# The inverse's turn written straight into four partitions per frequency, the taps' rows in another room, and a new front order

## The chip, the cores and the metric

The kernel runs on one core of a Trainium2 chip. Its engines are TensorE (PE, with PEld its weight loads), VectorE (DVE), ScalarE (ACT), GpSimd (POOL) and SyncE (SP, which here only issues transfers); 16 DMA engines carry transfers, which are issued from the queues of SP, POOL and ACT. SBUF has 128 partitions; TensorE writes its results to PSUM. The metric is the time of one execution in microseconds. The time before is 525.67 us, the median of three runs (524.36 to 526.06).

## The reference

For x of 2048 rows and 512 columns, the result is `g * a + (1 - g) * b`, with `g = sigmoid(x . gate_w)` for each row. `b` is a dense layer pair, `gelu(x w1 + b1) w2 + b2`, 512 to 1792 and back. `a` is a state-space convolution over the 2048 rows, column by column:

```python
logdA = dt * A                                   # dt = exp(log_dt)
P = jnp.exp(logdA[:, :, None] * l[None, None, :])
K = jnp.einsum("dn,dnl,dn->dl", Cc, P, dB).real  # taps, 512 x 2048
Kf = rfft(pad(K)); Uf = rfft(pad(u)); y = irfft(Uf * Kf)[:L]
a = y + u * Dskip
```

All inputs are float32.

## The kernel before, in words

The program has two halves. The **front** computes three things side by side: the dense layers (`hidden`, then `output`, each product as three passes of a number split into a high and a low part), the 512 x 2048 taps (`taps`: `prepare`, `powers`, `magnitudes`, `rotate`, and the products of `contract` into pk), and the first stage of the transform of the input and of the taps (`first_stage`). The results of the first stages go to two arrays in DRAM, tu_d (input) and tk_d (taps): 32 blocks of 256 KB each, one for each of 32 frequencies k0. The last eighteen of the dense products of `output` (of three matmuls each) are put aside in `late`.

The order of the front's instructions on every engine is made by a planner (`Plan.run`): each task has a duration, what it reads and writes, and a due time; of the tasks that are ready on an engine the one with the earliest due time is issued. Due times come from the constants at the top of the file (T_0 and T_MLP for the dense layers, K_0 and T_KG for the taps, T_EARLY, T_LOFT and T_DEN for the loads of tu_d, and many offsets D_...), so a changed constant moves instructions on all engines.

`early` issues, at the end of the front, loads of the first tu_d blocks into rooms that the front leaves free: 8 columns of den (the room in which the taps' powers lie), 11 of attic and 8 of loft, 27 in all.

The **back** (`conv`) is written out by hand, in program order. In sixteen steps s it takes two frequencies n = 2s and 2s + 1 each: `signal` (products p2u from the tu_d rows), `taps` (products p2k from the tk_d rows, copied by ACT into k), `product` (six operations on DVE into v), `inverse` (products pa) and `turn`. `turn` copies pa to one of six tiles sa on ACT, and then has to change the layout: the last products (pb) contract over all frequencies, so that each frequency's result, [128 partitions = 2 parts c x 2 kinds x 32 q] x 512, must end up in only four partitions, with the 32 q beside each other. Before, SP writes sa to an array t_d in DRAM (t4_d in the code; 32 stores of 256 KB), and when a group of eight frequencies is there, POOL reads it back in pieces of 512 KB into 32 partitions that lie four apart: the first 8 columns q into den, the other 24 into the tile t3. The pieces of the last group are issued by ACT. The last pieces of the first two groups are held back until step 9, because their place in t3 serves for tk_d rows until then; other tk_d rows lie in a ring of eight tiles tk.

`dense` reads the dense layers' share of the output back from DRAM, 512 KB each, six times on SP in steps 7 to 12 and twice on ACT behind the last step. `rest` issues the late dense products (L1244 to L1246): three of them in step 15, the other fifteen behind the last inverse. Then come the products pb (L1304), the gate and the addition, on DVE or, for six of sixteen rows blocks, on ACT and POOL, and the stores to the output.

Of the kernel before, what the change touches and what calls it, by code (L numbers as in the profile page):

```python
# [9 lines left out]
F32 = mybir.dt.float32  # L10
# [7 lines left out]
P = 128  # L18
# [15 lines left out]
T_0 = 21.909  # L34
T_MLP = 406.545
K_0 = 31.523
T_KG = 356.763
U_0 = 28
U_GAP = 18
LAG = 12.856  # L40
TABLE = 19.14
D_KA = -33.555
D_KP = -84.187
D_S1 = 23.678
D_EV = -33.402
D_H = -65.365
D_LO = -21.589
PS = (2, 3, 1, 2)
N_ACC, N_H, N_PK, N_PU = PS
D_SP = 2.869  # L50
MEM = (6, 2, 3)
N_LD, N_HL, N_ST = MEM
D_XS = -168.313
D_G = 1.725
N_WARM = 13
T_EARLY, T_LOFT, T_DEN = 405.144, 330.334, 535.529
Y_K, Y_U = 43.23, 26.971
W_MLP = (-0.0644, -0.031, 0.0179)
W_KG = (-0.0422, -0.0319, -0.0259)
W_U = (-0.0349, -0.1398, -0.0169)  # L60
D_MAG = -0.166
D_ROT = 0.588
D_CON = 0.043
D_PHA = 0.289
D_PRE = -2.671
D_XL = 25
D_COE = -3.439
D_OUT = -2.679
N_REST = 3
D_KA0 = 0  # L70
D_DT = 19
D_PRM = -248.822
D_D0 = -601.022
D_WAVE0 = -266.408
D_COE0 = -24.094
D_SP1 = -464.705
D_G0 = 1
D_GW = 522.519
D_XS0 = 74.778
T_PRE = 0  # L80
W_CAST = (0, 0, 0, 0, 0, 0, 0, 0, 1, 1, 0, 1, 0, 0)
X_CAST = (1, 0, 1, 0)
D_X0, D_B2, D_B2C = -1509.465, -139.804, -674.499
# [30 lines left out]
def seat(n, c, kind):  # L114

    return 4 * (16 * kind + 2 * (n % 8) + c) + n // 8
# [11 lines left out]
def constants():  # L128
# [39 lines left out]
    g2 = np.zeros((32, 64, 32, 2))  # L168
    for n, k in enumerate(ko):
        er, ei = om(4 * np.outer(q - 31.5, k + 32 * k1) + (q - 31.5)[:, None])  # L170
        f2[n, 0], f2[n, 1] = er, -ei
        a = 2.0 * np.pi * (k + 32 * k1 + 0.25) / L
        g2[n, :, :, 0] = np.cos(np.outer(a, m))
        g2[n, :, :, 1] = np.sin(np.outer(a, m))
        g2[n, :, 0, 1] = 1 - 2 * (k1 % 2)
# [20 lines left out]
TURN_PE = 0.095  # L196

# [22 lines left out]
class Plan:  # L220
# [26 lines left out]
    def run(self, fixed=None):  # L247
# [13 lines left out]
        for _ in self.tasks:  # L261
# [25 lines left out]
            if t.wire:  # L287
                took, (before, behind) = t.wire
                wire = max(wire, at + before) + took
                end = wire + behind  # L290
                if p == "SP":
                    lanes.append(end)
# [13 lines left out]
def gated_mix(  # L306
# [7 lines left out]
    logdt0: bass.AP,  # L314
# [17 lines left out]
    t4_d = dr.tile([4, 2, GROUP, 2, 32, D], F32, name="t4_d")  # L332
# [11 lines left out]
    def places(attic, loft, den):  # L344

        rooms = [attic[:, k] for k in range(N_ATTIC)] + [loft[:, k * D : k * D + D] for k in range(N_LOFT)]
        return [den[:, k] for k in range(N_DEN)] + rooms + rooms[: 32 - N_US]

    def front(pool, psum, keep, attic, loft, den):
# [39 lines left out]
        pr = pool.tile([P, 6, UW], F32, name="pr")  # L389
        dtb = pool.tile([P, UW], F32, name="dtb")  # L390
# [72 lines left out]
        def early():  # L463

            us = places(attic, loft, den)
# [3 lines left out]
            for n in range(N_US):  # L469
                m = n - N_DEN  # L470
                if m < 0:
                    due, key = T_DEN + n, [("xc", n // 4)]
                elif m < N_ATTIC:
                    due, key = T_EARLY + 2.5 * m, [keys[m]]
                else:
                    due, key = T_LOFT + m, ["xt", "xv"] if m < N_ATTIC + 4 else ["tt"]
# [7 lines left out]
        def make_dt(x, k, r, ki, key, due, load, store):  # L484
# [20 lines left out]
            move(180 if n < UW else 84, load, due - 1, [], [key], hold=0.65 if n < UW else 0.4)  # L505
            vec(4 * (n + 130), before, due, [], [key])
            act(n, lambda: nc.scalar.activation(r, r, AF.Exp, scale=0.25), due, [], [key], table="exp")
            vec(6 * (n + 130), behind, due, [], [key] if store is r else [key, "dtb"])

        def first_dt():  # L510

            x, k, r, ki = (loft[:, 2048 + UW * m : 2048 + UW * m + UW] for m in range(4))
            make_dt(
                x, k, r, ki.bitcast(I32), "tt", D_D0,
                lambda: nc.sync.dma_start(x, logdt0), dtb,
            )

        def other_dts():
# [3 lines left out]
            make_dt(  # L522
                x, k, r, ki.bitcast(I32), "dt", D_DT,
                lambda: nc.sync.dma_start(x, logdt.rearrange(shape, c=4)), r,
            )
# [25 lines left out]
        def prepare(u, t, eb_k):  # L551
# [4 lines left out]
            move(393, lambda: nc.sync.dma_start(pr, prm[u]), t - 20 if u else D_PRM, [], ["pr"])  # L556
            if u:
                move(
                    66, lambda: nc.gpsimd.dma_start(dtb, dt_d[:, sl].to_broadcast([P, UW])), t - 20,
# [88 lines left out]
        def waves(t):  # L648
# [4 lines left out]

            act(99 * CW, sines, t + D_KA, ["ph"], ["tt"], "sin", ops=3)

# [62 lines left out]
        def contract(u, c, k, t):  # L718
# [45 lines left out]
            for h in range(8):  # L764
# [9 lines left out]
                move(448, store, t + 5, [("sk", i, j) for i in range(2) for j in range(4)], [], out=True, hold=0.65)  # L774
# [93 lines left out]
        def dots(b, t):  # L868

            for n in range(2 * b, 2 * b + 2):  # L870
                xd, key = load(xs[n], t - 10)
                vec(
                    512,
# [6 lines left out]
        def gates(b0, b1_, t):  # L880
# [12 lines left out]
            vec(100, sides, t + D_LO, [], keys)  # L893
# [46 lines left out]
        def hidden(i, t):  # L940
# [24 lines left out]
            def gelu():  # L965
# [10 lines left out]
                ops=nf + 2,  # L976
# [7 lines left out]
        def output(i, t):  # L984
# [19 lines left out]
            for s in range(2):  # L1004
                if b == NB - 1 or i == 4 * NB - 6:
# [6 lines left out]
                    0.2295 * n, lambda s=s, q=q: products(s, acc[q]), t + LAG + D_OUT * (j == 3),  # L1012
# [21 lines left out]
        def dense():  # L1034
# [23 lines left out]
            move(20, lambda: nc.sync.dma_start(dm[0:P:32], dskip), -80, [], ["dm"], hold=0.65)  # L1058
# [63 lines left out]
    def conv(pool, ps, late, attic, loft, den):  # L1122
# [4 lines left out]
        us = places(attic, loft, den)  # L1127
# [73 lines left out]
        def turn(s):  # L1201

            for n in (2 * s, 2 * s + 1):
                sa = sas[n % 6]
                nc.scalar.copy(sa, pas.pop(n))
# [16 lines left out]
        held = []  # L1222

        def dense(k, on):

            q = HERE.index(k) if k in HERE else 6 + THERE.index(k)
            r = 5 + 2 * q if q < 7 else 0
# [5 lines left out]
            on.dma_start(mos[k], out[2 * k : 2 * k + 2].rearrange("s p d -> p s d"))  # L1233
# [15 lines left out]
        for n in range(N_TK):  # L1249
# [3 lines left out]
            if n == 1:  # L1253
                t3 = pool.tile([P, 24, D], F32, name="t3", bufs=1)
# [6 lines left out]
        for s in range(16):  # L1261

            for n in range(2 * s + N_TK + (2 if s else 0), 2 * s + N_TK + 4):
                if n < 24:
                    fetch(n if n < 16 else n + 8)
            if s == 0:
                for n in range(16, 24):
                    fetch(n)
            if s in (2, 4, 6, 8):
                consts(s // 2 + 3)  # L1270
            for n in range(2 * s + N_ROOM, min(2 * s + N_ROOM + 2, 32)) if s > 3 else ():
# [8 lines left out]
            if s == 9:  # L1280
                for to, rows in held:
# [121 lines left out]
```

## Time and profile before

| What | us |
|---|---|
| median of three runs | 525.67 |
| lowest and highest | 524.36, 526.06 |
| the profiled execution's own time | 527.21 |
| its span, first to last instruction | 525.4 |
| PE busy | 504.2 (96%) |
| PEld busy | 387.0 (74%) |
| DVE busy | 428.7 (82%) |
| ACT busy | 351.5 (67%) |
| POOL busy | 42.1 (8%) |
| DMA: bytes moved | 107.87 MB, 205 GB/s over the span |

The mean granted clock of TensorE is 0.986. The front lasts to about 412 us, the back from there. A matmul's end is modelled, so PE's busy time says that it had work in flight, not that it was at its peak; the idle times between are what to look at. Line numbers in the page are those of the kernel before; in the changed kernel the same statements stand 10 to 45 lines earlier.

### The profile page before, as it was taken

How to read it: one execution, taken by the hardware profiler on the slowest of the kernel's cores; microseconds unless marked ns; L12 is line 12 of the kernel's file. 1: busy time of each engine (PE TensorE's matmuls, PEld its weight loads, DVE VectorE, ACT ScalarE, POOL GpSimd, SP SyncE). 2: the span in 40 equal slices, each digit the busy share in tenths (PEclk: the TensorE clock that was granted, in tenths of full speed). 3: DMA queues.
4: the chain of work that ended last, by engine and by line, in shares of the span. 5: the costliest groups of instructions: out<-in, count | busy, mean ns of one | idle time of the engine just before them, and what ended most of it. 6: DMA issues, size and time to landing. Idle time of an engine off the chain costs nothing.

```text
span 525.4 us, 12205 instructions
## 1 busy us (share of the span) xinstructions
PE 504.2 (96%) x4810; PEld 387.0 (74%) x4810; DVE 428.7 (82%) x793; ACT 351.5 (67%) x626; POOL 42.1 (8%) x81
## 2 busy tenths in 40 slices
PE   6999998999999999999999999899999699999995
PEld 6897887799888989888898887778889542222451
DVE  6899989999999997979999899599931177777643
ACT  5798754899884789885686996556644346565311
POOL 2000000000000000002000020001010000110113
PEclk8899999999999999999999999999999899999999
DMA  8867784251684233538462267782388978999978
GB/s 293 327 226 235 262 297 145 81 203 51 186 223 141 81 110 125 193 128 192 91 203 42 81 161 198 165 301 42 113 234 197 291 252 319 354 346 388 343 285 310
DMA packets 80128, 107.87 MB, mean 205 GB/s; under 512 B 39396, under 2 KB 40680, under 8 KB 79528
## 3 DMA queue, kind: packets, MB, share of 16 engines
q1 hardware_dynamic: 74056, 85.10, 50.1%
q0 software_dynamic: 5088, 18.59, 13.3%
q10 hardware_dynamic: 928, 3.41, 1.8%
q8 instruction: 38, 0.62, 0.5%
q14 instruction: 18, 0.15, 0.1%
HBM read 61.46 MB, written 45.62 MB: 204 GB/s over the span
## 4 chain that ended last, share of the span: by engine, by line
PE 72%; ACT 8%; DMA 8%; DVE 8%; SPq 2%; issue 1%; ACTq 0%; DVEq 0%
PE pk L728 9%; PE ph L950 7%; PE ph L952 7%; PE ph L951 7%; PE acc L998 7%; PE acc L999 6%; PE acc L1000 6%; PE p2u L1160 6%; PE p2k L1160 6%; PE pa L1199 3%; DMA tu_d<-attic 3%; PE pb L1304 3%; PE ph L435 2%; DMA attic<-in_xs_dram 2%; SPq L769 2%; ACT ph L967 2%
## 5 line engine op out<-in xcount | busy, mean ns | idle before, releaser
L950 PE MATMUL ph<-xh,wh 128*128 128x256 f32 x448 | 129.2, 288 | 2.2 <-ACT wh L828 2.0
L952 PE MATMUL ph<-xh,wl 128*128 128x256 f32 x448 | 128.2, 286 | 1.2 <-DVE wl L830 1.2
L951 PE MATMUL ph<-xlo,wh 128*128 128x256 f32 x448 | 127.9, 286 | 0.0
L950 PEld LDWEIGHTS ph<-xh,wh 128*128 128x128 f32 x448 | 86.4, 193 | 9.9 <-issue 5.4
L951 PEld LDWEIGHTS ph<-xlo,wh 128*128 128x128 f32 x448 | 86.5, 193 | 2.1
L952 PEld LDWEIGHTS ph<-xh,wl 128*128 128x128 f32 x448 | 86.5, 193 | 1.4 <-DVE wl L830 1.4
L998 PE MATMUL acc<-wh,hh 128*128 128x512 f32 x206 | 82.8, 402 | 2.3 <-ACT hh L970 2.3
L1000 PE MATMUL acc<-wh,hl 128*128 128x512 f32 x206 | 80.9, 393 | 0.5 <-DVE hl L980 0.5
L999 PE MATMUL acc<-wl,hh 128*128 128x512 f32 x206 | 80.9, 393 | 0.0
L967 ACT ACTIVATE ph<-ph,b1t 128x256 f32<-128x256 f32 x112 | 50.4, 450 | 43.2 <-PE ph L952 41.3
L728 PE MATMUL pk<-y,den 128*32 128x64 f32 x2048 | 61.6, 290 | 1.2 <-DVE y L714 1.2
L728 PEld LDWEIGHTS pk<-y,den 128*32 128x32 f32 x2048 | 57.2, 136 | 5.5 <-issue 3.5
L980 DVE TENSOR_TENSOR hl<-ph,hh 128x512 fp32r<-128x512 f32 (+1 forms) x62 | 38.2, 618 | 25.3 <-ACT hh L970 24.9
L998 PEld LDWEIGHTS acc<-wh,hh 128*128 128x128 f32 x206 | 38.7, 188 | 17.5 <-issue 7.2
L691 DVE TENSOR_TENSOR y<-y,ea 128x64 f32<-128x64 f32 (+4 forms) x80 | 45.3, 566 | 3.5 <-ACT y L681 3.0
L1000 PEld LDWEIGHTS acc<-wh,hl 128*128 128x128 f32 x206 | 38.7, 188 | 10.3 <-DVE hl L980 1.6
L999 PEld LDWEIGHTS acc<-wl,hh 128*128 128x128 f32 x206 | 38.7, 188 | 6.3
L534 DVE TENSOR_TENSOR loft<-den,zz 128x256 f32<-128x256 f32 (+2 forms) x48 | 37.3, 777 | 1.1 <-ACT den L660 0.6
L970 ACT CAST hh<-ph 128x512 fp32r<-128x512 f32 (+1 forms) x62 | 33.0, 533 | 7.3 <-PE acc L999 5.5
L1168 ACT COPY k<-p2k 128x512 f32<-128x512 f32 x32 | 18.8, 586 | 28.6 <-issue 13.1
L535 DVE TENSOR_TENSOR loft<-den,zz 128x256 f32<-128x256 f32 (+2 forms) x48 | 37.1, 773 | 0.0
L703 DVE TENSOR_TENSOR y<-y,loft 128x2048 f32<-128x2048 f32 x16 | 36.6, 2285 | 0.0
(193 smaller groups left out, 880.1 us busy)
## 6 DMA issues: line engine op xcount, KB each, us to landing
tu_d<-attic SPq DMA_DIRECT2D x64, 128.0 KB, 3.5
tk_d<-sk SPq DMA_DIRECT2D x32, 256.0 KB, 4.9
t_d<-sa SPq DMA_DIRECT2D x32, 256.0 KB, 5.1
tk<-tk_d SPq DMA_DIRECT2D x24, 256.0 KB, 4.9
t<-t_d POOLq DMA_DIRECT2D x9, 512.0 KB, 6.4
attic<-in_xt_dram SPq DMA_DIRECT2D x16, 256.0 KB, 4.5
attic<-in_xs_dram SPq DMA_DIRECT2D x16, 256.0 KB, 4.9
xh_d<-xh SPq DMA_DIRECT2D x8, 512.0 KB, 3.8
```

Of the source, the lines that this page charges most:

```text
L534: vec(2 * m, lambda: vv.tensor_mul(t, a, br), due, [ka, *kb], [kt])
L691: nc.vector.tensor_mul(both(n, 64 - 3 * n, n), both(0, 64 - n, n), an)
L728: nc.tensor.matmul(pks[q][32 * j : 32 * j + 32, :, gg], x[:, r, :, ch], y[:, r, :, ch], start=(r == 0), stop=(r == 1), skip_group_check=True,)
L950: nc.tensor.matmul(p, h, xh[xk][:, d], start=(d == 0), stop=False)
L951: nc.tensor.matmul(p, h, xlo[xk][:, d], start=False, stop=False)
L952: nc.tensor.matmul(p, lo, xh[xk][:, d], start=False, stop=(d == 3))
L967: nc.scalar.activation(phs[q][:, n], phs[q][:, n], AF.Gelu_apprx_tanh, bias=b1t[:, f : f + 1])
L980: nc.vector.tensor_sub(lo, phs[q][:, 0:nf], hi.bitcast(F32))
L998: nc.tensor.matmul(a, h, wh[1][w], start=start, stop=False)
L999: nc.tensor.matmul(a, h, wl[1][w], start=False, stop=False)
L1000: nc.tensor.matmul(a, l, wh[1][w], start=False, stop=(j == 3))
L1160: nc.tensor.matmul(out[64 * i : 64 * i + 64], w, x, start=True, stop=True)
```

## The change

- `turn`: after ACT's copy, POOL issues one transfer for each frequency n, from sa straight into t3, partitions n, n + 32, n + 64 and n + 96, all 32 columns q of 2 KB, so 64 KB in each of the four partitions. t4_d, the groups of eight, the pieces held back and ACT's pieces are gone; t3 has all 32 columns. The matrices g1 and g2 are laid out to fit (`seat`, and the order of kind and q).
- The tk_d rows lie in den, eight columns in turn; the ring tk and the use of t3 for them are gone. A row for step s + 4 is issued in step s.
- `early` has 19 loads of tu_d, not 27 (none into den). The other 13 are issued in the steps 0 to 6 on SP, two a step.
- `dense`: all eight reads are issued by SP in the steps 7 to 14; none on ACT.
- Front: the first unit's dt comes as a seventh row of the parameters' load (448 KB) instead of one of its own (64 KB); Dskip's load is issued by POOL instead of SP; the planner has other due times, some other durations, a factor on transfers behind its 22nd us and one new offset, D_LAST.

The arithmetic is the same; TensorE has as many matmuls in each group as before.

```diff
-T_0 = 21.909
-T_MLP = 406.545
-K_0 = 31.523
-T_KG = 356.763
+T_0 = 22.399
+T_MLP = 408.543
+K_0 = 32.114
+T_KG = 350.709
...
-T_EARLY, T_LOFT, T_DEN = 405.144, 330.334, 535.529
+T_EARLY, T_LOFT = 345.94, 385.15
...
-HERE, THERE = (7, 6, 0, 1, 2, 3), (4, 5)
-N_DEN = 8
-N_ROOM = N_ATTIC + N_LOFT
-N_US = N_DEN + N_ROOM
-
-GROUP = 8
+PAIRS = ((7, 13), (6, 15), (0, 17), (1, 0), (2, 2), (3, 4), (4, 6), (5, 8))
+N_US = N_ATTIC + N_LOFT
...
 def seat(n, c, kind):
 
-    return 4 * (16 * kind + 2 * (n % 8) + c) + n // 8
+    return 32 * (2 * c + kind) + n
...
         def fetch(n):
-            if 16 <= n < 24:
-                t2s[n] = t3[:, n]
-            else:
-                t2s[n] = pool.tile([P, D], F32, tag="tk", name=f"tk{n}", bufs=N_TK)
+            t2s[n] = den[:, n % N_TK]
             nc.sync.dma_start(t2s[n], tk_d[ko[n]])
...
             for n in (2 * s, 2 * s + 1):
                 sa = sas[n % 6]
                 nc.scalar.copy(sa, pas.pop(n))
-                g, k = divmod(n, GROUP)
-                nc.sync.dma_start(t4_d[g, :, k].rearrange("e c q d -> (c q) e d"), sa)
-                if k < GROUP - 1:
-                    continue
-                rows = t4_d[g].rearrange("e k c q d -> (e k c) q d")
-
-                for h in (0, 4, 8, 16, 24) if g == 3 else (0, 8, 16, 24):
-                    if h == 24 and g < 2:
-                        held.append((t3[g:P:4, 16:24], rows[:, 24:32]))
-                        continue
-                    on = nc.gpsimd if n < 31 else nc.scalar
-                    e = h + (4 if g == 3 and h < 8 else 8)
-                    to = t3[g:P:4, h - 8 : e - 8] if h > 7 else den[g:P:4, h:e]
-                    on.dma_start(to, rows[:, h:e])
+                nc.gpsimd.dma_start(t3[n:P:32], sa)
...
-            for n in range(2 * s + N_TK + (2 if s else 0), 2 * s + N_TK + 4):
-                if n < 24:
-                    fetch(n if n < 16 else n + 8)
-            if s == 0:
-                for n in range(16, 24):
-                    fetch(n)
+            for n in range(2 * s + N_TK, min(2 * s + N_TK + 2, 32)):
+                fetch(n)
...
-            for n in range(2 * s + N_ROOM, min(2 * s + N_ROOM + 2, 32)) if s > 3 else ():
+            for n in range(2 * s + N_US, min(2 * s + N_US + 2, 32)):
                 nc.sync.dma_start(us[n], tu_d[ko[n]])
...
-            if s == 9:
-                for to, rows in held:
-                    nc.gpsimd.dma_start(to, rows)
...
-            if 7 <= s < 13:
-                dense(HERE[s - 7], nc.sync)
-        for k in THERE:
-            dense(k, nc.scalar)
+            if 7 <= s < 15:
+                dense(*PAIRS[s - 7])
```

How the instructions stand now, at three places. In the back, POOL's queue before (den and t_4779 are the two parts of the target, 32 partitions with 4096 numbers each):

```order
L1030 DMA out_dram<-io_145 128x512
L1219 DMA den<-t_d 32x4096
L1219 DMA t_4779<-t_d 32x4096 x2
L1219 DMA den<-t_d 32x4096
L1219 DMA t_4779<-t_d 32x4096 x2
L1282 DMA t_4779<-t_d 32x4096 x2
```

and POOL's queue in the changed kernel at the same place (sa_4754 to sa_4759 are the six tiles sa; 4x32x512 is four partitions, 32 columns q, 512 numbers):

```order
L1019 DMA out_dram<-io_143 128x512
L1192 DMA t_4766<-sa_4754 4x32x512
L1192 DMA t_4766<-sa_4755 4x32x512
L1192 DMA t_4766<-sa_4756 4x32x512
L1192 DMA t_4766<-sa_4757 4x32x512
L1192 DMA t_4766<-sa_4758 4x32x512
L1192 DMA t_4766<-sa_4759 4x32x512
```

POOL had twelve reads of 512 KB and now has 32 transfers of 256 KB, each behind ACT's copy of its frequency; SP's stores to t_d are gone. At the passage from front to back, SP's queue before (L769 stores the last taps to tk_d, L478 is `early`, L1141 fetches tk_d rows):

```order
L478 DMA loft<-tu_d 128x512
L478 DMA den<-tu_d 128x512
L769 DMA tk_d<-sk 64x16x64 x8
L478 DMA loft<-tu_d 128x512
L478 DMA den<-tu_d 128x512
L1133 DMA cc_4773<-in_c_dram 128x384
L1141 DMA tk_4775<-tk_d 128x512
```

and in the changed kernel:

```order
L471 DMA attic<-tu_d 128x512 x11
L471 DMA loft<-tu_d 128x512 x7
L757 DMA tk_d<-sk 64x16x64 x8
L471 DMA loft<-tu_d 128x512
L1122 DMA cc_4762<-in_c_dram 128x384
L1127 DMA den<-tk_d 128x512 x2
```

The eight loads into den no longer stand around the stores, and the fetches go to den. On ACT, between the last copies into sk (behind the last first-stage products) and the first copy of the back, before (L967 and L970 finish a block of hidden products):

```order
L754 COPY sk<-pu_92 128x64x8
L967 ACTIVATE ph_89<-ph_89,b1t 128x256
L970 CAST hh_139<-ph_89 128x256
L967 ACTIVATE ph_87<-ph_87,b1t 128x256 x2
L970 CAST xh_106<-ph_87 128x512
L1019 ACTIVATE io_144<-acc_85,gate 128x512
```

and in the changed kernel:

```order
L742 COPY sk<-pu_91 128x64x8
L955 ACTIVATE ph_87<-ph_87,b1t 128x256 x2
L958 CAST hh_138<-ph_87 128x512
L955 ACTIVATE ph_88<-ph_88,b1t 128x256
L958 CAST hh_137<-ph_88 128x256
L955 ACTIVATE ph_86<-ph_86,b1t 128x256 x2
L958 CAST xh_104<-ph_86 128x512
L1008 ACTIVATE io_142<-acc_84,gate 128x512
```

One more block of hidden products (two activations and a cast) is finished behind the taps' last first stage than before; on TensorE 120 hidden matmuls stand behind those products, before it were 108.

More of the change, by code (lines that the diff above doesn't have):

```diff
@@ L288, in run @@
                 took, (before, behind) = t.wire
[L289 removed]
+                wire = max(wire, at + before) + took * (SLOW if at > 22.0 else 1.0)
                 end = wire + behind
@@ L342, in gated_mix, with places @@
     c1t = cp.tile([P, 64], F32, name="c1t")
-    def places(attic, loft, den):
+    def places(attic, loft):
         rooms = [attic[:, k] for k in range(N_ATTIC)] + [loft[:, k * D : k * D + D] for k in range(N_LOFT)]
-        return [den[:, k] for k in range(N_DEN)] + rooms + rooms[: 32 - N_US]
+        return rooms + rooms[: 32 - N_US]
     def front(pool, psum, keep, attic, loft, den):
@@ L463, in early @@
         def early():
-            us = places(attic, loft, den)
+            us = places(attic, loft)
             keys = [("ux", 0)] + [("st", k) for k in range(N_ST)]
@@ L503, in behind @@
                 v.tensor_mul(store, r, ki.bitcast(F32))
[L505 to L508, printed above, removed]
+            vec(4 * (n + 130), before, due, [], keys)
+            act(n, lambda: nc.scalar.activation(r, r, AF.Exp, scale=0.25), due, [], keys[:1], table="exp")
+            vec(6 * (n + 130), behind, due, [], keys)
         def first_dt():
[L512 to L516, printed above, removed]
+            k, r, ki = (loft[:, 2048 + UW * m : 2048 + UW * m + UW] for m in range(3))
+            move(459, lambda: nc.sync.dma_start(pr, prm[0]), D_PRM, [], ["pr", "dtb"])
+            make_dt(dtb, k, r, ki.bitcast(I32), ["tt", "dtb"], D_D0, dtb)
         def other_dts():
@@ L772, in store @@
                     )
-                move(448, store, t + 5, [("sk", i, j) for i in range(2) for j in range(4)], [], out=True, hold=0.65)
+                move(450, store, t + 5, [("sk", i, j) for i in range(2) for j in range(4)], [], out=True, hold=0.65)
         def taps():
@@ L1126, in conv @@
         zs = [pool.tile([P, D], F32, name=f"z{k}", bufs=1) for k in range(2)]
-        us = places(attic, loft, den)
+        us = places(attic, loft)
         ko = k0_order()
```

139 lines of the change are left out of this document (66 added, 73 removed).

## The prediction

> **What bounds the kernel now.** I read the windows by stage first, because shares over the whole span mix a front and a back with different limits. Columns: stretch, its length, busy time and count of PE, PEld, DVE, ACT and POOL, the granted clock, the DMA engines' busy share, GB/s.
>
> ```profile
> 380.00:400.00 20.00, 20.00 (x245) 17.61 (x244) 6.61 (x7) 8.62 (x17) 1.78 (x2) 1.00 0.79 227
> 400.00:420.00 20.00, 15.74 (x102) 13.64 (x103) 2.93 (x5) 8.12 (x17) 1.72 (x2) 0.88 1.01 258
> 420.00:440.00 20.00, 20.00 (x99) 7.80 (x97) 14.65 (x24) 10.13 (x19) 0.00 (x0) 0.95 0.85 297
> 460.00:480.00 20.00, 20.00 (x110) 5.36 (x108) 16.33 (x27) 11.58 (x22) 2.57 (x5) 1.00 0.97 354
> 480.00:500.00 20.00, 20.00 (x102) 8.84 (x103) 12.01 (x20) 8.54 (x16) 2.04 (x4) 1.00 1.01 364
> 510.00:525.40 15.40, 9.69 (x46) 3.02 (x42) 6.00 (x8) 2.94 (x5) 6.38 (x5) 0.97 0.84 322
> ```
>
> TensorE is busy without a break from 420 to about 520, at full clock from 440, and the DMA engines are nearly as full. The one hole is between 400 and 420: 4.26 us idle, and a lower clock behind it. The chain of waits (start, us, what) then shows what fills the back half:
>
> ```profile
> 396.25 0.61 SPq L769
> ...
> 404.75 5.21 DMA tk_d<-sk
> 410.04 6.44 DMA tk<-tk_d
> 416.61 4.25 PE p2k L1160 x8
> 420.86 2.32 PE p2u L1160 x8
> 423.18 1.72 PE p2k L1160 x8
> 424.90 1.72 PE p2u L1160 x8
> ...
> 428.33 1.02 PE pa L1199 x8
> 429.35 1.87 PE p2u L1160 x8
> 431.22 1.72 PE p2k L1160 x8
> 432.93 1.02 PE pa L1199 x8
> ...
> 505.81 13.91 PE pb L1304 x64
> 519.74 0.75 DVE attic L1316
> ```
>
> One of the sixteen steps is 432.93 - 428.33 = **4.60 us**, and makes two turns (two frequencies, 256 KB each), so a turn must be carried off every 2.3 us. No link between 416.61 and 519.74 is a transfer: the turn by DRAM is wholly hidden today, the last part by the late dense products ahead of pb. So its removal cannot shorten this stretch; only a slower turn can lengthen it. A direct turn therefore has nothing to win here, and the question is what it costs.
>
> **The turn's price.** Two stretches in which few kinds of transfer run, in the same columns, and the last wide-open transfers by issue (KB each, median us from issue to landing):
>
> ```profile
> 460.40:464.40 4.00, 4.00 (x24) 1.27 (x24) 3.08 (x6) 2.48 (x5) 0.00 (x0) 1.00 1.06 404
> 90.40:91.40 1.00, 1.00 (x44) 1.00 (x40) 1.00 (x5) 1.00 (x1) 0.00 (x0) 1.00 0.92 205
> ```
>
> ```profile
> 84.80 5.47 SPq L456 DMA_DIRECT2D tu_d<-attic  x8
> 91.45 1.28 SPq L821 DMA_DIRECT2D attic<-in_xt_dram  x2
> ```
>
> ```profile
> t_d<-sa SPq DMA_DIRECT2D x32, 256.0 KB, 5.1
> xh<-xh_d POOLq DMA_DIRECT2D x8, 512.0 KB, 3.9
> den<-t_d POOLq DMA_DIRECT2D x3, 512.0 KB, 4.5
> ```
>
> From 460.40 the queue carries only transfers with 128 partitions at the SBUF end: 404 GB/s at a share of 1.06, or 404 / (16 x 1.06) = 23.8 GB/s for a busy engine. From 90.40 it carries the last of the eight stores of L456, which read 64 neighbouring partitions each (SP issues nothing between 90.27 and 91.45): the engines are just as busy, and move 205 GB/s, 13.9 each. So which partitions a transfer touches can halve its rate. It is not the count alone: 512 KB into 32 partitions four apart (den) took 4.5 us, against 3.9 for 128 (xh). A price in proportion to the partitions (205 x 4/64 = 13 GB/s, 20 us a turn) is excluded by that pair.
>
> [...]
>
> No row shows a transfer whose far end is four partitions 32 apart with 64 KB for each, so the price is bounded:
> - from below, by bytes: 256 KB at 404 GB/s is 0.65 us, and it is hidden as now (term 0);
> - if each of the four partitions is filled by one engine at a time: 4 x 23.8 = 95 GB/s, 2.75 us;
> - the same with engines at the halved rate: 4 x 13.9 = 56 GB/s, 4.7 us.
> A transfer that ends in only four places is nearest to the second and third, and turns of neighbouring steps overlap in part. I take **3.6 us**, a little under their middle.
>
> What is behind it: ACT's copy (L1191) of frequency n writes one of six sa tiles and so waits for turn n - 6 to have landed; behind it on ACT stand the k copies of the taps (L1154), for those PE's p2k banks, and PE's next pa. So once the turns are slower than 2.3 us each, PE falls to their pace, and pb, which contracts over all 128 partitions, waits for the last. The sum by landings: the first copies start here
>
> ```profile
> 429.41 1.07 ACT L1205 COPY sa<-pa 128x512 f32<-128x512 f32 x2 [0.40 <-DMA t<-tk_d]
> 384.06 1.78 POOL L1030 DMA_DIRECT2D out_dram<-io  x2 [6.70 <-ACT io L1019]
> ```
>
> 12.8 us behind the first p2k. With 0.6 for the copy and 2 for the tail of a landing, the last turn lands 15.4 + 32 x 3.6 = 130.6 us behind the first p2k; pb starts 505.81 - 416.61 = 89.2 behind it now. **+41 us**; at 2.75 it is 15.4 + 88 - 89.2 = +14, at 4.7 it is +77. POOL's issue (0.89 us each, 32 of them) lies beside this. SP loses 32 stores (some 1.2 us of queue a step) in front of which it waited for ACT each step; nothing on the path waits for SP there, so 0.
>
> **The other parts.** *Taps' rows in den.* Same bytes; now fetched two steps (9.2 us) ahead against 4.9 us to land, where eight more lay ready before. Hidden at the present rate, part of the +41 if the turns block the engines; if bare, some 2 us at the first steps. The 8 further tu_d rows that no longer have den move behind 416 into six of the steps, 2 MB there: hidden, since they are asked for nine steps ahead.
>
> *The hole at 412.* These rows carry it:
>
> ```profile
> 392.61 0.64 PE L435 MATMUL ph<-s,c1t 32*64 32x512 f32 x2
> ...
> 416.61 2.55 PE L1160 MATMUL p2k<-tk,cc 128*64 128x512 f32 x4 [4.26 <-DMA tk<-tk_d]
> ```
>
> ```profile
> 396.25 9.49 SPq L769 DMA_DIRECT2D tk_d<-sk  x8
> 405.78 1.43 SPq L478 DMA_DIRECT2D loft<-tu_d  x1
> 407.26 1.00 SPq L478 DMA_DIRECT2D den<-tu_d  x1
> ```
>
> From the last first-stage products to the first p2k is 24.0 us, of which PE has dense work for all but 4.26; then eight p2k take 4.25 us instead of 1.72 and eight p2u 2.32 instead of 1.72, at the lower clock: 3.1 us more. In the new order one more group of twelve hidden matmuls stands behind that point (+1.4 us of cover), and the den loads are gone from SP's queue around the eight stores (2 MB, 5 us at 404 GB/s). I count 3.3 of the idle time and 1.7 of the clock as won: **-5**, bounds -7.4 and 0.
>
> *The front plan.* PE's waits between 40 and 400 us, from the list of waits:
>
> ```profile
> PE acc L998 <- ACT hh L970: 2.3, 1, 2.3
> PE ph L435 <- DVE hl L980: 2.1, 1, 2.1
> PE pk L728 <- DVE y L714: 1.2, 1, 1.2
> ```
>
> 5.6 us with the work unchanged, so a new order can win at most that, and lose as much by the same kind of misses: 0, bounds -5.6 and +5.6. The first dt now waits for a 448 KB load instead of 64 KB (+1 us at 404 GB/s), beside dense work with its weights still arriving: 0.
>
> **Sum.** 525.4 (the span) - 5 + 41 + 0 = 561.4. The profiled execution took 527.2, 1.8 more than its span, and the median of the runs is 525.67, 0.3 over the span; so **561.7 us**. Own range of this case: 525.7 - 7 + 14 = 533 to 525.7 - 5 + 77 = 598.
>
> **Rivals.**
> - *Hidden by bytes (faster).* All sixteen engines fill the four partitions at the usual rate; then turns land in some 5 us, the copies never wait, and only the hole counts: 525.7 - 5 = **520.7**. For it: 32 partitions cost hardly more than 128, and the DMA share of 0.97 to 1.01 drops as 8.4 MB of reads go. Against it: the halved rate at 90.40, and that a turn ends in an eighth as many partitions as den's loads. It decides when a turn costs under 2.3 us. 0.23.
> - [...] 0.08.
> - *Hidden turn, lost front.* The turns cost nothing, but den's fetches come two steps ahead behind tu_d rows and the new front idles where the old one did not: -5 + 5 = 0, **525.7**, with as much chance of a few us above. 0.05 within 0.3%, 0.03 above.
> - *Turns bound, as forecast:* 0.61.
>
> About 0.3% (1.6 us) is what a measurement of this kernel can tell from no change. Faster: 0.23; same 0.05; slower 0.61 + 0.08 + 0.03 = 0.72. The range from 518 to 592 leaves out the top of the slower case, the serial rival and the better half of the faster one, some 0.2.
>
> **What would show it.** Right: the direct turns' issues land in well over 5 us, growing; ACT's sa copies wait for a DMA of sa (nothing of the kind above 0.4 us now); a step of pa to pa of 6 to 8 us instead of 4.60; PE idle ahead of p2k or pa between 430 and 530; GB/s in the back half far under 354 at a DMA share near 1; pb's first matmul waiting for the last t<-sa. The hole before the first p2k is under 2 us, and the eight p2k behind it take under 3 us. Wrong: steps still 4.60 us with the DMA share below 0.9, and pb right behind L1245's last product; then the price per turn was the term that failed. If the turns are hidden and the time is still not below 524, the front's order failed. If the steps stretch but PE waits for den's rows rather than ACT for sa, the place of the mechanism was wrong.

## The result, and the profile after

The changed kernel takes **642.55 us** (median of four runs, 639.09 to 650.55), against 525.87 for the kernel before beside it: a ratio of **1.2149 (95% interval 1.2081 to 1.2218)**. One run of each kernel (650.55 and 533.24) was slow, over 1.5% above its fastest, and the ratio leaves both out. The profiled execution took 639.09 us with a span of 637.1.

By the terms of the prediction, from the two chains of waits: the first p2k comes at 410.06 instead of 416.61 (-6.6 us); from there to pb it takes 205.8 us instead of 89.2 (+116.6); pb and what follows take 21.3 instead of 19.6 (+1.7). Together 525.4 + 111.7 = 637.1.

The chain of waits of the changed kernel (start, us, what), its beginning and its end:

```profile
410.06 1.08 PE p2k L1146 x4
411.14 1.72 PE p2u L1146 x8
...
418.01 1.02 PE pa L1185 x8
...
549.68 12.29 issue
562.65 33.34 DMA t<-sa
596.96 18.41 DMA t<-sa
615.83 15.47 PE pb L1265 x64
631.32 0.75 DVE loft L1277
```

The hole before the first p2k is closed, and the first four p2k take 1.08 us instead of 2.55, at a granted clock of 1.00 from 400 to 420 instead of 0.88. But the end of the back is now two turns, of 33 and 18 us. The windows (stretch, length, busy time and count of PE, PEld, DVE, ACT and POOL, granted clock, DMA share, GB/s) show the stage between:

```profile
420.00:440.00 20.00, 15.56 (x82) 4.10 (x78) 14.73 (x24) 7.13 (x14) 4.08 (x6) 0.95 0.93 97
440.00:460.00 20.00, 9.73 (x27) 2.13 (x28) 3.68 (x6) 4.10 (x9) 2.67 (x4) 0.67 1.08 120
460.00:480.00 20.00, 12.62 (x42) 2.85 (x40) 6.27 (x11) 5.15 (x10) 2.67 (x4) 0.78 1.09 118
480.00:500.00 20.00, 10.18 (x28) 2.29 (x30) 3.55 (x7) 3.06 (x6) 1.33 (x2) 0.66 1.10 114
600.00:605.00 5.00, 0.00 (x0) 0.00 (x0) 0.00 (x0) 0.00 (x0) 0.00 (x0) 0.50 0.97 53
```

The DMA engines are fuller than before (1.08 to 1.10, before 0.92 to 1.01) and move a third as much: 114 to 120 GB/s where the stretch from 460 to 480 had 354. From 600 to 605, when only the last turns run and no engine computes, a share of 0.97 moves 53 GB/s. From 440 to 500 TensorE issues 27 to 42 matmuls in 20 us, before 102 to 110.

The transfers by issue (KB each, median us from issue to landing), and the two queues of the stretch 420 to 600 (packets, MB, share of 16 engines; q0 is POOL's, q1 SP's):

```profile
den<-tk_d SPq DMA_DIRECT2D x32, 256.0 KB, 25.8
t<-sa POOLq DMA_DIRECT2D x32, 256.0 KB, 30.3
```

```profile
q1 hardware_dynamic: 7035, 12.77, 58.6%
q0 software_dynamic: 8163, 7.86, 47.2%
```

A turn takes 30.3 us, and the taps' rows, which have nothing to do with it, take 25.8. SP's queue moved 12.77 MB in 0.586 x 16 x 180 us, **7.6 GB/s for a busy engine**; POOL's 5.8. In the kernel before, from 415 to 505, they were 22.6 and 21.6:

```profile
q1 hardware_dynamic: 12606, 22.45, 68.9%
q0 software_dynamic: 576, 6.29, 20.2%
```

Who waits for it in the back (engine, line, what it waited for: us in total, how many times, the longest):

```profile
POOL t L1192 <- ACT sa L1191: 171.9, 20, 19.0
...
PE p2k L1146 <- DMA den<-tk_d: 46.6, 11, 10.1
ACT sa L1191 <- DMA t<-sa: 37.0, 7, 19.1
...
PE pb L1265 <- DMA t<-sa: 26.6, 1, 26.6
```

Both ways stand here: ACT waits for a free sa, and PE for the taps' rows. POOL's 171.9 us are no cause: it waits for ACT's copy, which waits in turn.

### The profile page after: what moved, and what is told of

Same layout as the page of the kernel before. It is cut to its first block, busy times and chain, and to the rows that moved or that the text cites. A ratio compares the mean times of both kernels' runs of the same rounds, so it can differ in the third digit from the quotient of the medians.

```text
span 637.1 us, 12173 instructions
## 1 busy us (share of the span) xinstructions
PE 535.1 (84%) x4810; PEld 389.0 (61%) x4810; DVE 427.2 (67%) x792; ACT 349.6 (55%) x625; POOL 57.9 (9%) x102
## 4 chain that ended last, share of the span: by engine, by line
PE 54%; issue 21%; DMA 10%; DVE 6%; ACT 5%; POOL 2%; SPq 0%; POOLq 0%; DVEq 0%; ACTq 0%
PE pk L716 8%; DMA t<-sa 8%; PE ph L938 7%; PE ph L940 6%; PE ph L939 6%; PE acc L986 6%; PE acc L988 6%; PE acc L987 6%; PE pb L1265 2%; POOL t L1192 2%; PE ph L431 2%; DVE wl L818 1%; DMA tu_d<-attic 1%; PE p2k L1146 1%; DMA sk<-in_w_dram 1%
## 5 line engine op out<-in xcount | busy, mean ns | idle before, releaser
L938 PE MATMUL ph<-xh,wh 128*128 128x256 f32 x448 | 127.9, 285 | 4.6 <-DVE hl L968 3.9
L939 PE MATMUL ph<-xlo,wh 128*128 128x256 f32 x448 | 126.6, 283 | 0.0
L938 PEld LDWEIGHTS ph<-xh,wh 128*128 128x128 f32 x448 | 85.1, 190 | 12.2 <-issue 6.8
L940 PEld LDWEIGHTS ph<-xh,wl 128*128 128x128 f32 x448 | 85.1, 190 | 2.3 <-DVE wl L818 2.3
L939 PEld LDWEIGHTS ph<-xlo,wh 128*128 128x128 f32 x448 | 85.1, 190 | 1.9
L1168 DVE TENSOR_TENSOR v<-p2u,k 128x512 f32<-128x512 f32 x16 | 11.1, 691 | 102.7 <-PE p2u L1146 93.1
L1146 PE MATMUL p2k<-den,cc 128*64 128x512 f32 x64 | 35.5, 765 | 52.1 <-DMA den<-tk_d 46.6
L1146 PEld LDWEIGHTS p2k<-den,cc 128*64 128x64 f32 x64 | 6.9, 160 | 73.7 <-issue 43.8
L1191 ACT COPY sa<-pa 128x512 f32<-128x512 f32 x32 | 17.7, 588 | 45.4 <-DMA t<-sa 37.0
## 6 DMA issues: line engine op xcount, KB each, us to landing
den<-tk_d SPq DMA_DIRECT2D x32, 256.0 KB, 25.8
t<-sa POOLq DMA_DIRECT2D x32, 256.0 KB, 30.3
```

The costliest lines, as they stand in the source:

```text
L938: nc.tensor.matmul(p, h, xh[xk][:, d], start=(d == 0), stop=False)
L939: nc.tensor.matmul(p, h, xlo[xk][:, d], start=False, stop=False)
L940: nc.tensor.matmul(p, lo, xh[xk][:, d], start=False, stop=(d == 3))
L1146: nc.tensor.matmul(out[64 * i : 64 * i + 64], w, x, start=True, stop=True)
```

## The experiments

"Placing" below means which four of the 128 partitions a frequency's turn fills; g1 is laid out to fit by `seat`, and all else stays the changed kernel's. A "group" is four neighbouring partitions, 4i to 4i + 3. "GB/s for a busy engine" is always a queue's bytes divided by the time that its packets kept engines busy.

### Neighbouring frequencies in different groups of four partitions

```diff
-    return 32 * (2 * c + kind) + n
+    return 32 * (2 * c + kind) + slot(n)
+def slot(n):
+    return 4 * (n % 8) + n // 8
...
-                nc.gpsimd.dma_start(t3[n:P:32], sa)
+                nc.gpsimd.dma_start(t3[slot(n):P:32], sa)
```

> The changed kernel with one thing altered: frequency n is written to the partitions p, p+32, p+64, p+96 with p = 4(n mod 8) + n div 8 in place of p = n, so that eight frequencies in a row lie in eight different groups of four neighbouring partitions (the last matrix's rows follow). Same bytes, same queue, same number of transfers. Theory A (turns hinder each other because neighbouring frequencies end in the same few partitions' way into SBUF): turns that are open together no longer meet, 256 KB land in 5 to 10 us instead of 30, the copies into sa hardly wait, and only the front's gain is left: 515 to 522 us. Theory B (a transfer into four partitions is slow by itself, whichever they are, some 5.9 us each one after another): 635 to 650 us as before.

Measured: 566.74 us (564.42 to 570.92), ratio 1.0752 (1.0676 to 1.0829). The edit changes nothing but the partitions' numbers, and takes off some 76 of the 117 us; the rest stays, so the time lies between the bands of theories A and B, and neither holds alone. Landings fall from 30.3 to 18.0 us for a turn and from 25.8 to 15.7 for the taps' rows:

```profile
440.00:460.00 20.00, 14.36 (x44) 3.21 (x46) 4.83 (x8) 5.56 (x11) 2.00 (x3) 0.74 1.08 180
```

180 GB/s instead of 120 at the same share. So where the four partitions lie decides most of it here. In this placing a row at p and one at p + 32 are still filled side by side.

### Two groups in turns

```diff
-    return 4 * (n % 8) + n // 8
+    return 4 * (2 * (n // 8) + n % 2) + n % 8 // 2
```

> As the spread placing, but frequencies in a row alternate between only two groups of four partitions (p = 4(2(n div 8) + n mod 2) + (n mod 8) div 2). Theory A: two groups are open at a time instead of one, so the price of a turn falls from 5.9 to some 3 us; the last turn lands some 15 + 96 us behind the first product of the back instead of 205, 535 to 570 us. Theory B: 635 to 650 us.

Measured: 580.88 us, a single run: between the two placings, but 11 us above the top of what was expected. Of each 32 partitions, eight neighbouring frequencies fill two groups instead of eight (before this edit), and 14 us are lost again.

### The same turns on ACT's queue

```diff
-                nc.gpsimd.dma_start(t3[slot(n):P:32], sa)
+                nc.scalar.dma_start(t3[slot(n):P:32], sa)
```

> The spread placing, with the 32 turns issued on ACT's queue (right behind the copy, which is on ACT too) instead of POOL's. If only the partitions matter (theory A), within 5 us of the spread kernel. [...]

Measured: 599.31 us, a single run: 33 us more than with the same placing on POOL's queue (566.74), so the partitions are not all that matters.

```profile
460.00:480.00 20.00, 10.99 (x48) 2.64 (x48) 7.37 (x12) 6.09 (x11) 0.00 (x0) 0.76 0.56 133
```

```profile
q1 hardware_dynamic: 5498, 9.85, 40.6%
q10 hardware_dynamic: 2151, 4.28, 18.4%
```

(The queues are those from 420 to 520; q10 is ACT's.) From 460 to 480 the engines are 0.56 full on average (1.09 on POOL's queue), and yet TensorE issues 48 matmuls in these 20 us, in the kernel before 110. That a few of the sixteen engines carried all the turns while the rest idled is a guess from these shares and was not shown: no view here tells the engines apart.

### The turn by DRAM again, all else as changed

```diff
-                nc.gpsimd.dma_start(t3[n:P:32], sa)
+                g, k = divmod(n, 8)
+                nc.sync.dma_start(t4_d[g, :, k].rearrange("e c q d -> (c q) e d"), sa)
+                if k < 7:
+                    continue
+                rows = t4_d[g].rearrange("e k c q d -> (e k c) q d")
+                for h in (0, 4, 8, 16, 24) if g == 3 else (0, 8, 16, 24):
+                    on = nc.gpsimd if g < 3 else nc.scalar
+                    e = h + (4 if g == 3 and h < 8 else 8)
+                    on.dma_start(t3[g:P:4, h:e], rows[:, h:e])
```

> The changed kernel with its new front, den for the taps' rows and loads of the input's rows as they are, but with the turn by DRAM as before (stores of 256 KB on the SP queue, reads of 512 KB into 32 partitions four apart, the last group's on the ACT queue), into the one tile of 32 columns. Both theories: the turn is hidden again and the time shows what the rest of the change is worth. From the changed kernel's trace the first inverse product stands 10.3 us earlier than before (418.0 against 428.3), so 514 to 518 us; if the transfers' extra load in the back slows the fetches that now come only two steps ahead, 520 to 526.

Measured: 526.85 us (524.35 to 529.04), ratio 0.9987 (0.9957 to 1.0017): the kernel before's time, with the hole closed; that is a little above the second range of the expectation. So the direct turn alone is worth 1.2149 / 0.9987, some 114 us; and the front's gain is given back. Where: TensorE's groups with their idle time, and the chain:

```profile
L1147 PE MATMUL p2k<-den,cc 128*64 128x512 f32 x60 | 18.8, 615 | 4.8 <-DMA den<-tk_d 4.5 <-ACT f L1136 0.3
L1274 PE MATMUL pb<-t,g1t 128*64 128x512 f32 x64 | 14.2, 594 | 1.5 <-DMA t<-t_d 1.5
```

```profile
461.52 11.46 DMA den<-tk_d
...
485.06 10.77 DMA attic<-out_dram
495.89 6.39 DMA t_d<-sa
```

The fetch at 461.52 is issued by SP behind two stores of sa (460.01 and 460.26) and a dense read (460.92), and the stores wait for ACT's copies of their step. The wide turn below shows the same fetches without these stores.

### The changed placing, with little other traffic

```diff
             for n in range(2 * s + N_TK, min(2 * s + N_TK + 2, 32)):
-                fetch(n)
+                t2s[n] = den[:, n % N_TK]
...
-            for n in range(2 * s + N_US, min(2 * s + N_US + 2, 32)):
-                nc.sync.dma_start(us[n], tu_d[ko[n]])
```

> The changed kernel, its placing untouched, but in the back half the rows of the taps from the ninth frequency on and the rows of the signal from the twentieth on are not fetched (the rows that lie there already are used again; what is computed from them is not the reference's, the instructions on PE, ACT and DVE are the same). So 37 of SP's transfers of 256 KB are gone and the turns have the engines almost to themselves; beside them only the dense outputs' 4 MB. [...] Theory B (the turns are slow in themselves by 5.9 us whatever else runs): span 632 to 640.

Measured: 619.95 us, span 617.8, a single run. This is the price in dispute with little beside it (the dense outputs' 4 MB stay).

```profile
409.57 1.08 PE p2k L1146 x4
...
569.49 25.36 DMA t<-sa
595.43 16.11 PE pb L1263 x64
```

pb starts 185.9 us behind the first p2k, (185.9 - 15.4) / 32 = **5.33 us a turn**, 49 GB/s, with 37 of SP's transfers gone. With them it was (205.8 - 15.4) / 32 = 5.95. So 0.6 us a turn, some 20 us in all, are these 37 transfers; the rest is the turns' own price. The span lies 14 us below theory B's band (632 to 640).

### One turn's four partitions four apart

```diff
-    return 32 * (2 * c + kind) + n
+    return base(n) + 4 * (2 * c + kind)
+def base(n):
+    return 16 * (0, 1, 4, 5, 2, 3, 6, 7)[n % 8] + n // 8
...
-                nc.gpsimd.dma_start(t3[n:P:32], sa)
+                nc.gpsimd.dma_start(t3[base(n) : base(n) + 13 : 4], sa)
```

> The changed kernel with another placing of the same four partitions per frequency: they now lie four apart inside a block of sixteen, so that the four rows of one turn belong to four different neighbouring groups of four partitions, and frequencies that follow each other take different blocks. One transfer per turn as before, on the same queue, 256 KB. [...]

Measured: 541.8 us (540.44 to 546.79), ratio 1.0254 (1.0202 to 1.0306): some 25 us off the spread placing, with a turn landing in 13.0 us and a row of the taps in 12.1. Again only numbers of partitions changed. From 410 to 500:

```profile
q1 hardware_dynamic: 8696, 15.42, 68.9%
q0 software_dynamic: 6475, 6.29, 34.1%
```

That is 15.5 GB/s for a busy engine on SP's queue and 12.8 on POOL's (from 7.6 and 5.8), and still not the 22.6 and 21.6 of the kernel before.

> The placing on four different groups per turn, and the same 37 fetches left out as in the run before it. Theory A: turns land in 3 to 6 us, PE is never held up by a transfer, span 505 to 514 (the front's gain of some 11 us kept). Theory B: turns still 10 us or more; if they are hidden at all the pace is above 4.6 us a step and the span over 530.

With the same 37 fetches left out (the diff is the two before this together): 525.44 us, span 523.3, a single run, and neither theory's span held. The turns still land in 10.1 us, as theory B had it, and late turns near 471 hold up ACT and then PE for 2.6 us, at a granted clock of 0.83 in this stretch:

```profile
480.00:500.00 20.00, 17.44 (x63) 10.09 (x60) 4.44 (x7) 2.83 (x5) 4.02 (x6) 0.83 0.68 144
```

and POOL's queue from 410 to 500:

```profile
q0 software_dynamic: 8710, 8.45, 46.4%
```

So a turn into four partitions costs something even when its four lie four apart, those of the three turns behind it in other blocks of sixteen, and little else runs: 8.45 MB in 46.4% of 16 x 90 us, 12.6 GB/s for a busy engine, the same as with SP's traffic.

### A turn into 128 partitions

This run and the next weigh two theories. D: the few target partitions cost the rate (12.8 GB/s for a busy engine with the four of them four apart). S: a transfer from SBUF to SBUF is slow by itself.

```diff
-                nc.gpsimd.dma_start(t3[n:P:32], sa)
+                nc.gpsimd.dma_start(t3[:, n], sa)
```

> The changed kernel, except that a turn goes from the 128 partitions of sa into 128 partitions (one column of the 64 KB tile) instead of four. It leaves out the transposition that the turn is for; bytes, queue, count of transfers, waits and the arithmetic's amount are the changed kernel's. [...]

Measured: 518.14 us, span 516.1, a single run; theory S falls. (The kernel leaves out the transposition, so this is a price and no result to be had.) The queue's bytes, count of transfers and waits are those of the changed kernel, and from 410 to 500 its engines move 23.7 GB/s each:

```profile
q1 hardware_dynamic: 9012, 16.07, 52.1%
q0 software_dynamic: 2562, 8.39, 24.6%
...
t<-sa POOLq DMA_DIRECT2D x32, 256.0 KB, 5.0
```

Between the first p2k and pb, PE waits 0.8 us in all, and for no transfer. So these transfers from SBUF to SBUF are not slow (5.0 us to land), and neither are den's fetches beside them (6.2): of the changed kernel's 642.55 us some 124 are the price of aiming at four partitions instead of 128, with all that hangs on it (which four they are, and into how many packets a transfer is cut). The fetches run here as late in the program as in the run with the turn by DRAM, and the engines are as full (a share of 1.00 to 1.02 from 430 to 470); but no store of sa stands before them on SP's queue. The last goes out at 459.4, 17 us ahead of the last p2k (476.7). In the run by DRAM it went out at 475.2, 11 us ahead (486.0), with landings of up to 11.6 us.

### By DRAM, but into the four partitions

The placing is that with a turn's partitions four apart. SP stores sa to DRAM as it lies, and POOL reads the 256 KB from there into the same four partitions, 64 KB each.

```diff
+    t_d = dr.tile([32, P, D], F32, name="t_d")
...
-                nc.gpsimd.dma_start(t3[base(n) : base(n) + 13 : 4], sa)
+                nc.sync.dma_start(t_d[n], sa)
+                nc.gpsimd.dma_start(t3[base(n) : base(n) + 13 : 4], t_d[n])
```

> [...] Theory D: the read into four places runs at the same 13 GB/s per engine, lands in 10 us or more, and the stores come on top: 555 to 580. Theory S: the read from DRAM runs at 20 GB/s or more per engine, lands in 4 to 8 us: 525 to 535, as with the regrouped turn by DRAM.

Measured: 595.19 us, a single run; above both bands, with one sign of each. POOL's engines moved 3.96 MB in 13.0% of 16 x 90 us, 21 GB/s each (theory S), but the turns' reads took 10.8 us to land (theory D) and den's rows 16.5, with the engines two thirds full:

```profile
440.00:460.00 20.00, 8.98 (x38) 2.90 (x34) 5.68 (x10) 3.84 (x9) 2.01 (x4) 0.74 0.66 214
```

Here source and target are 64 KB in one piece, so there is a new theory: the piece holds up what stands behind it on its engine. With this edit the rows in DRAM lie 4 KB apart with 2 KB used, and each partition is filled from 32 separate rows:

```diff
-    t_d = dr.tile([32, P, D], F32, name="t_d")
+    t_d = dr.tile([32, P, 2 * D], F32, name="t_d")
...
-                nc.sync.dma_start(t_d[n], sa)
-                nc.gpsimd.dma_start(t3[base(n) : base(n) + 13 : 4], t_d[n])
+                nc.sync.dma_start(t_d[n, :, 0:D], sa)
+                nc.gpsimd.dma_start(t3[base(n) : base(n) + 13 : 4], t_d[n, :, 0:D])
```

> [...] Theory H (the one piece of 64 KB holds up whatever stands behind it on its engine for some 3 us): the rows of den land in 5 to 8 us, the waits on stores of sa of 14 us go, 524 to 540 us. Theory N (writing four partitions is what holds up the rest, in whatever pieces): landings of 12 us and more, 565 to 600 us.

Measured: 555.21 us (553.73 to 556.33), ratio 1.0503 (1.0456 to 1.0549). It lies between the two bands. The pieces were worth some 40 us (den's rows 9.9 us instead of 16.5, the engines full again), but the rest stays:

```profile
440.00:460.00 20.00, 15.76 (x64) 4.47 (x64) 9.37 (x16) 6.47 (x12) 3.68 (x6) 0.91 1.07 292
```

With DRAM as the source the four partitions fill at 15.3 GB/s for a busy engine (5.34 MB in 24.3% of 16 x 90 us), a little above the 12.8 from SBUF.

### Can the front's gain be kept?

From the turn by DRAM with the changed front (526.85 us), the dense outputs' loads later:

```diff
-            if 7 <= s < 15:
-                dense(*PAIRS[s - 7])
+            if 11 <= s < 15:
+                dense(*PAIRS[2 * s - 22])
+                dense(*PAIRS[2 * s - 21])
```

> The turn by DRAM as before with the changed kernel's front (526.85 us, the front's gain given back to waits for the taps' rows while the engines' share is 1.0 from 430 to 485 and 0.6 to 0.76 from 500 to 520), and one change: the eight loads of the dense outputs, 512 KB each, come two per step from the twelfth step on instead of one per step from the eighth, when the taps' rows are all asked for. Theory T (the front's gain is lost only because these loads delay the taps' rows): PE's waits for den's rows fall from some 4.5 us and the cold clock behind them goes, 517 to 522 us, faster than both kernels. Theory U (the sum of the bytes binds, whatever the order): the waits move to the turns of the last steps and to pb, 525 to 529.

Measured: 528.73 us (525.03 to 530.25), ratio 0.9997 (0.9970 to 1.0024). Theory T falls: PE's waits for den's rows go from 4.5 us to 2.7 only. The first of them in the chain stands at 440, before any dense load is issued, and the late part moved to the turns:

```profile
440.33 11.65 DMA den<-tk_d
...
486.75 8.41 DMA t_d<-sa
495.23 7.68 DMA t_d<-sa
503.17 2.95 DMA t<-t_d
```

That leaves the back's own plan of fetches. The last run keeps the changed front (constants, parameters' load, Dskip's queue, planner's costs) and takes the whole back of the kernel before, eight signal rows in den and the ring tk included:

```diff
+T_DEN = 535.529
 T_EARLY, T_LOFT = 345.94, 385.15
...
-    return 32 * (2 * c + kind) + n
+    return 4 * (16 * kind + 2 * (n % 8) + c) + n // 8
...
-            t2s[n] = den[:, n % N_TK]
+            if 16 <= n < 24:
+                t2s[n] = t3[:, n]
+            else:
+                t2s[n] = pool.tile([P, D], F32, tag="tk", name=f"tk{n}", bufs=N_TK)
             nc.sync.dma_start(t2s[n], tk_d[ko[n]])
...
-                nc.gpsimd.dma_start(t3[n:P:32], sa)
+                g, k = divmod(n, GROUP)
+                nc.sync.dma_start(t4_d[g, :, k].rearrange("e c q d -> (c q) e d"), sa)
+                if k < GROUP - 1:
+                    continue
...
```

> The changed kernel's front plan with the whole back of the kernel before: the turn by DRAM, 27 rows of the signal ahead, eight of them again in the room of the powers (den), the taps' rows in rooms of their own and in the columns of the tile that the turn fills last. So only the front plan's part of the change is left. Theory T (the front plan wins 6.5 us at the first p2k, and the back of before, with less to fetch late, can keep it): first p2k near 410 to 412, PE busy from 420 to 505, 517 to 521 us, faster than both kernels. Theory U (the gain belonged to den being free: with den's eight loads back in the queue ahead of the taps' rows the hole returns, or the engines, full from 430 on, give it back): first p2k at 414 or later or PE idle for 5 us and more behind it, 523 to 529 us.

Measured: **518.91 us** (517.83 to 520.76), ratio **0.9818 (0.9781 to 0.9855)**: 1.8% below the kernel before, and faster than both kernels. TensorE's waits between 40 and 400 us, which were 2.3, 2.1, 1.2, 0.6 and 0.3, are now

```profile
PE ph L947 <- DVE hl L977: 1.1, 1, 1.1
PE acc L990 <- ACT io L1017: 0.4, 1, 0.4
PE acc L997 <- DVE hl L977: 0.3, 1, 0.3
```

and the hole is 2.4 us instead of 4.26, at a clock of 0.91 instead of 0.88. Behind it PE is busy without a break to the end of the inverse:

```profile
400.00:420.00 20.00, 17.58 (x98) 10.44 (x98) 6.89 (x12) 9.41 (x19) 1.72 (x2) 0.91 0.92 268
...
440.00:460.00 20.00, 20.00 (x108) 5.49 (x109) 15.90 (x26) 11.77 (x23) 1.60 (x3) 1.00 1.02 366
460.00:480.00 20.00, 20.00 (x106) 5.59 (x104) 15.79 (x26) 11.13 (x22) 3.10 (x6) 1.00 0.99 364
```

The change in three parts, each from ratios to the kernel before:

| Part | ratio | some us of 526 |
|---|---|---|
| front plan alone | 0.9818 | -10 |
| and the back's other changes: taps' rows in den, 19 signal rows ahead instead of 27, all dense reads on SP | 0.9987 | +9 |
| and the direct turn as placed | 1.2149 | +114 |

## Why the prediction was wrong

The direction, the cause and most of the signs were right; the time (561.7, range 518 to 592) was 81 us too low, and a step of two turns, 6 to 8 us in the text, came to 2 x 5.95 = 11.9. By its steps:

- **What bounds the kernel.** Right: the turn by DRAM was hidden, so its removal had nothing to win. The turn written wide, at no cost to the path, gave 518.14, which is what the front alone gives (518.91).
- **The price per turn, 3.6 us: the step that failed.** It measured 5.95 us, above the upper bound of 4.7 too. Of that 5.33 are the turns themselves (the run with little other traffic), 0.6 SP's transfers. (Both keep the prediction's 15.4 us of head. Its 2 us for the tail of a landing no run shows: the shortest landing of a store of sa before took 2.4 us, and the last turn of the changed kernel 18.4. The first copy came 9.0 us behind the first p2k and not 12.8, with the clock at 1.00 from 400 to 420 instead of 0.88; with that they are 6.07 and 5.45.) I took the middle because "turns of neighbouring steps overlap in part". They hardly do: four neighbours lie in the same groups, and with up to six turns open the pace was still some 49 GB/s for all of them. Spreading them, with no other edit, took some 76 us off. The row at 90.40, at half the rate, had hinted that partitions share something; the prediction used it as a rate of one engine (13.9 GB/s) and not as a limit on all engines that work on the same groups at a time. The row alone could not show it, since its far end, 64 separate rows of 2 KB in DRAM, was another too; the placings show it (120 GB/s from 440 to 460 as changed, 180 when spread, at the same share of 1.08).
- **The serial rival** (0.08), turns wholly one after another at the upper bound of 4.7 us each, came nearest. Its price was too low by 1.25 us a turn, or by 0.63 with little other traffic (5.33). The placings fall into an order: four turns in a row in the same groups, 642.55; eight turns in a row in different groups, 566.74; the four partitions of a turn four apart instead of 32 and the next turns in other blocks of sixteen, 541.8. What lies behind this order no run shows, and it is not all: the engines of the last still moved 12.8 GB/s, those of wide turns 23.7.
- **Only the turns slow down: missing.** The sum had SP's transfers as hidden, "part of the +41 if the turns block the engines". The turns did block them: den's rows went from 4.9 to 25.8 us at 7.6 GB/s for a busy engine. So PE waits for the taps' rows (46.6 us) more than ACT for sa (37.0). The test that the prediction named for a wrong place of the mechanism is half met: both waits are there, and with the turns wide both are gone.
- **The hole, -5.** With the front plan's part in it, it measured -6.6 at the first p2k, and -10.3 at the first inverse product (418.01 instead of 428.33), where the clock's part is won too; the prediction had -5 for both. With den's eight loads back in place the hole is 2.4 us of idle time instead of 4.26, so closing it whole went with a den free of these loads, as the step said.
- **The front plan, 0 (bounds -5.6 and +5.6).** Too cautious: with the back of before, all of PE's listed waits fell from 6.5 us (5.6 in the three rows that the step counted) to 1.8, and front and hole together are worth some 10 us, twice the -5 that I counted.
- **Taps' rows in den, hidden.** Wrong with the turn by DRAM: there the back's other changes cost the whole gain, some 9 us. Full engines alone don't explain it, nor do the 13 signal rows beside the fetches instead of 5, for the wide turn had both, and PE waited for no row. What differs is that SP's stores of sa, and their bytes, are gone. Without them the last fetch goes out 17 us ahead instead of 11 (the prediction reckoned with two steps, 9.2 us); that SP no longer waits for ACT, which the prediction put at 0, may have been worth something. No run takes the stores off SP's queue and leaves their bytes, so the two are not separated. In the changed kernel all this is covered by the turns.
- **Hidden by bytes** (0.23) fell, and the test by the wide turn shows what it would have been: 518.14, against the 520.7 of the text. **Hidden turn, lost front** (0.05 and 0.03) fell too, since the turns cost much; only where the turn goes by DRAM again (526.85) is the gain lost.

## What to carry to other kernels

Price a transfer by the partitions that it and its neighbours in time fill, and not by its bytes alone: with 256 KB into four partitions instead of 128 a busy engine moved between 5.8 and 12.8 GB/s instead of 23.7, depending on which four, and SP's transfers slowed down with it. When rows of a layout may be permuted freely, as here by `seat`, spread them: rows written one after another four partitions apart instead of one took 642.55 us to 566.74, and the four of one transfer four apart instead of 32, with the next transfers in other blocks of sixteen, to 541.8. And test the parts of a change apart: here a front plan worth 1.8% lay hidden under a turn that cost some 22%.

## What the runs showed of the hardware that I had not expected

- The turns on POOL's queue set the rate of SP's transfers. SP's transfers, nearly all with 128 partitions, ran at 22.6 GB/s for a busy engine in the kernel before, at 15.5 beside turns into four partitions four apart, and at 7.6 beside the changed kernel's turns.
- Four partitions four apart still fill at only 12.6 GB/s for a busy engine, even with little else running, while 128 partitions take 23.7 from the same source. What holds it is open. The target alone does not: from DRAM the same four partitions took 15.3 in rows of 2 KB and 21 in one piece of 64 KB. POOL's queue moved those 8.45 MB in 8710 packets, and the wide turn's 8.39 MB in 2562; neither the number of packets nor the order in which a turn reads sa (32 partitions a row, the two kinds 32 apart) was varied by itself.
- One piece of 64 KB moves at 21 GB/s, but den's rows beside it took 16.5 us to land: the same transfer in rows of 2 KB was slower for itself (15.3 GB/s), let den's rows land in 9.9 us, and made the kernel 40 us faster (595.19 to 555.21).
